# Four more conversion rounds in the second layer's first slices, token forms four steps later, PSUM pools exchanged at the layer border

## The chip, the cores and the metric

The kernel runs on one core of one Trainium2 chip. The metric is the device time in microseconds (us) of one execution of the program. The core's engines are TensorE (PE, with its weight loads shown as PEld), VectorE (DVE), ScalarE (ACT), GpSimd (POOL) and SyncE (SP), which here only issues DMAs. Each engine works through its own instructions in the order in which the program issued them and waits at the head of that queue.

## What is computed

The reference is a causal linear attention with decay, followed by two feed-forward layers over its output:

```python
x = attn_out.transpose(0, 2, 1, 3).reshape(1536, 512)      # 1536 tokens, 512 features
h = x @ moe_w_in                                           # 512 x 2048
g = where(h >= 1, h, where(h <= -1, 0, (h + 1) ** 2 / 4))
x = g @ moe_w_out                                          # 2048 x 512
gate = 1 / (1 + exp(-(x @ moe2_w_gate)))                   # 512 x 1536
out = (gate * (x @ moe2_w_val)) @ moe2_w_out               # 1536 x 512
```

The layers' weights arrive as 64-bit floats.

## The kernel before, in words

**Attention** comes first (16 units, the loop at L910) and writes x as a high and a low part, `xh` and `xl`, so that a product is made of three matmuls: high by high, low weight by high, high weight by low. The 1536 tokens are three groups of 512, t = 0, 1, 2.

**Slices.** The first layer has 16 slices of 128 hidden features (n = 0 to 15), the second has 12 (n = 16 to 27). For a slice, `hidden` (L219, 12 matmuls) makes the hidden features of one token group in a PSUM bank h, ACT and DVE apply the activation, `parts` (L242) splits the result into gh (ACT) and gl (DVE), and `project` (L266, 12 matmuls) adds it to four output accumulators `accs`, one PSUM bank each. After the last slice of a group of slices `flush` (L291) takes the four accumulators into `part[t]` in SBUF, and only then are those banks free. Two pools of four PSUM banks serve this: "a" for the accumulators, "h" for hidden features and products (L958).

**Pairs.** From slice 4 on, slices 4 to 15 and 18 to 27 are worked in pairs n0, n1. Token groups 0 and 1 use a scheme with seven products where there would be eight (`pair_first` L455, `pair` L421; `product` L408 is six matmuls). It needs *token forms*, sums and differences of x (`forms_first` L370: ten DVE additions L381, then four `form_split`, each an ACT copy L367 and a DVE subtraction L368), and *weight forms* s31 and s24 (four additions L149, then `w_forms_split` L152: per form an ACT copy L156 and a subtraction L157). The weight forms are made on DVE in the first layer and on POOL in the second. Token group 2 is done by `hidden`. In the second layer one "pair" iteration (L607) handles the products of slice n0 (a) and n1 (b), projections and the two third-group slices: 14 products, 6 projections and 4 `hidden`, 84 + 72 + 48 = 204 matmuls. The second layer's first two slices, 16 and 17, are done without the scheme, for t = 0, 1, 2 in turn (the loop at L596): per slice and group two `hidden` and one `project`. Between the layers, `x_split` makes xh and xl of the second layer from `part`, and `forms_second` its token forms (DVE, L405).

**Conversion rounds.** There are 68 pieces of weights of 512 columns (two per first-layer slice, three per second-layer slice: two inputs and the output weights at column 1024). `w_round` (L164) is one round k: DVE finishes the bits of piece k-1 (`w_float`, L119, L123), ACT makes the high part of piece k-2 (`w_high`, L127), SP issues a load (`w_load`, L98, 512 KB into three raw buffers), ACT takes the words of piece k apart (`w_words`, L105, L112, L113), DVE makes the low part of piece k-2 (`w_low`, L131) and, where a piece completes a slice's inputs, the weight forms are begun (`w_forms`, L149). Pieces live in ten buffers; a round does nothing while piece k-12 is still needed (L176), nor while forms wait to be split and `prog["room"]` is false (L166). The first action of `w_round` after forms are made is to split them at its end. `w_need` makes rounds on the spot if a weight isn't ready; `pair` and `pair_first` call `w_forms_split` on the spot if forms aren't split (L425, L459). Nothing else paces the rounds: they stand where the program calls them, and that place sets how early a weight is ready.

**Order around the change.** `feed_forward` (L331) yields twice per slice and group. The main program (L961 to L973) takes 16 such steps after attention, and at each of the first 14 pops one entry of the list `made` of `forms_first`. Then come `first_layer` (L488), with three rounds spread over an iteration and one at its end, and `second_layer` (L583). In `second_layer`'s loop `go_on` (L321) runs one entry of `later` and makes a round unless that entry returns True: the rounds made there are two at t = 0, none at t = 1 (the `form_split` calls stand there) and two at t = 2.

Of the kernel before, what the change touches and what calls it, by code (L numbers as in the profile page):

```python
# [26 lines left out]
G0 = 4  # L27
# [13 lines left out]
def fused_kernel(ctx: ExitStack, tc: tile.TileContext, qkv, qd, cst, w1, w2, out):  # L41
# [279 lines left out]
    def go_on():  # L321

        if not (later and later.pop(0)()):
            w_round()
# [45 lines left out]
    def forms_first():  # L370


        at = lambda x, k, t: x[:, k * HK:(k + 1) * HK, t * TT:(t + 1) * TT].bitcast(F32)
        f = {}

        def forming(i, first, *terms):
            def one(k):
                if k == 0:
                    f[i] = fp.tile([P, HK, TT], F32, tag="s", name=f"f{i}")
                op, b_ = terms[k]  # L380
                dve.tensor_tensor(out=f[i], in0=f[i] if k else first, in1=b_() if callable(b_) else b_,  # L381
                                  op=op)
            return [lambda k=k: one(k) for k in range(len(terms))]

        add, sub = ALU.add, ALU.subtract
        both = lambda op, k, t: [(op, at(xh, k, t)), (op, at(xl, k, t))]
        yh, yl = [[at(x, k, 1) for k in range(2)] for x in (xh, xl)]
        return [
            *forming(0, yh[0], *both(sub, 0, 0), (add, yl[0])),
            *forming(3, yh[1], *both(sub, 0, 1), (add, yl[1])),  # L390
            *forming(1, yh[1], (sub, lambda: f[0]), (add, yl[1])),
            *forming(2, at(xh, 1, 0), (sub, lambda: f[1]), (add, at(xl, 1, 0))),
            lambda: form_split(f, 0),
            lambda: form_split(f, 1),
            lambda: form_split(f, 3),
            lambda: form_split(f, 2),
        ]
# [57 lines left out]
    def pair_first(n):  # L455

        w_need(n, 0)
        w_need(n + 1, 0)
        if n not in ready:  # L459
            w_forms_split(n)  # L460
        hw = HK * P
        g, v = ws[index[n, 0]], ws[index[n + 1, 0]]
        s31, s24 = ready[n]
        t_at = lambda i: (xt["h"][:, i], xt["l"][:, i])
        p0, p1, p2 = (bank(f"p{n}_{i}") for i in range(3))
        r = [rest(f"q{n}_{i}") for i in range(3)]
        product(p0, g, 0, x_at(0, 0), True)
        act.activation(r[0], p0, AF.Copy)
        yield
        product(p1, g, hw, x_at(1, 0), True)  # L470
        dve.tensor_tensor(out=r[0], in0=r[0], in1=p1, op=ALU.add)
        yield r
        product(p0, s24, 0, t_at(1), False)
        act.activation(r[1], p0, AF.Copy)
        yield
        product(p2, s31, hw, t_at(0), True)
        yield
        product(p0, s31, 0, x_at(0, 1), False)
        act.activation(r[2], p0, AF.Copy)
        dve.tensor_tensor(out=r[2], in0=r[2], in1=p2, op=ALU.add)  # L480
        yield
        product(p0, v, hw, t_at(2), False)
        yield p0
        product(p2, s24, hw, x_at(1, 1), False)
        dve.tensor_tensor(out=r[1], in0=r[1], in1=p2, op=ALU.add)
        yield

    def first_layer(waiting):  # L488

        square = lambda s: act.activation(s, s, AF.Square)  # L490
        for n0 in range(G0, NF1, GF):
            n1 = n0 + 1
            ending = n1 == NF1 - 1
            a = pair_first(n0)
            next(a)
            r = next(a)
            next(a)
            s11 = act1_begin(r[0], f"s{n0}_0")
            next(a)
            square(s11)  # L500
            next(a)
            act1_end(s11, r[0])
            s22 = act1_begin(r[2], f"s{n1}_1")
            project(*waiting[0], now=False)
            square(s22)
            g11 = parts(s11, n0, 0)
            act1_end(s22, r[2])
            w_round()
            project(*waiting[1], now=False)
            g22 = parts(s22, n1, 1)  # L510
            t_ = waiting[1][:2]
            flush(*t_, (0, 1))
            p0 = next(a)
            flush(*t_, (2, 3))
            s21 = act1_begin(p0, f"s{n1}_0")
            next(a)
            square(s21)
            act1_end(s21, p0)
            s12 = act1_begin(r[1], f"s{n0}_1")
            ha = hidden(n0, 2, 0)  # L520
            used.add(index[n0, 0])
            g21 = parts(s21, n1, 0)
            square(s12)
            act1_end(s12, r[1])
            w_round()
            project(n0, 0, g11, True, False)
            sa = act1(ha, n0, 2)
            act1_end(sa, ha)
            g12 = parts(s12, n0, 1)
            project(n1, 0, g21, False, True)  # L530
            w_round()
            hb = hidden(n1, 2, 0)
            used.add(index[n1, 0])
            if ending:
                x_split(0, (0, 1))
            project(n0, 1, g12, True, False)
            ga = parts(sa, n0, 2)
            sb = act1(hb, n1, 2)
            act1_end(sb, hb)
            gb = parts(sb, n1, 2)  # L540
            project(n1, 1, g22, False, True)
            w_round()
            if ending:
                x_split(0, (2, 3))
            waiting = [(n0, 2, ga, True, False), (n1, 2, gb, False, True)]
        return waiting

# [35 lines left out]
    def second_layer(waiting):  # L583

        x_split(1, range(4))
        f = forms_second()
        for p in waiting:
            project(*p)
        later.extend([
            lambda: x_split(2, (0, 1)),  # L590
            lambda: x_split(2, (2, 3)),
            lambda: form_split(f, 0) or form_split(f, 2) or True,
            lambda: form_split(f, 1) or form_split(f, 3) or True,
        ])
        fresh = None
        for t in range(NTT):  # L596
            for n in range(NF1, NF1 + GF):
                r = single(n, t)
                if fresh:
                    behind.append(fresh[:2] + (parts(fresh[2], *fresh[:2]),) + fresh[3:])  # L600
                if len(behind) == 2:
                    project(*behind.pop(0))
                fresh = n, t, r, n == NF1, n == NF1 + GF - 1
                go_on()
        behind.append(fresh[:2] + (parts(fresh[2], *fresh[:2]),) + fresh[3:])
        waiting = behind
        for n0 in range(NF1 + GF, NF1 + NF2, GF):  # L607
            n1 = n0 + 1
            a, b = pair(n0), pair(n1)
            next(a)  # L610
            w_round()
            for _ in range(4):
                next(a)
            prog["room"] = False
            for p in waiting:
                w_round()
                project(*p, now=False)
            flush(p[0], p[1], (0, 1))
            ra, ga = next(a), {}
            flush(p[0], p[1], (2, 3))  # L620
            prog["room"] = True
            xa = pair_act(n0, ra, ga)
            for _ in range(5):
                next(b)
                next(xa)
            w_round()
            project(n0, 0, ga[0], True, False)
            w_round()
            rb, gb = next(b), {}
            ha = single(n0, 2, pair_act(n1, rb, gb))  # L630
            w_round()
            project(n1, 0, gb[0], False, True)
            ha = parts(ha, n0, 2)
            w_round()
            hb = single(n1, 2)
            w_round()
            project(n0, 1, ga[1], True, False)
            hb = parts(hb, n1, 2)
            project(n1, 1, gb[1], False, True)
            waiting = [(n0, 2, ha, True, False), (n1, 2, hb, False, True)]  # L640
        for p in waiting:
            project(*p)
# [313 lines left out]
    with tc.manual_schedule():  # L956
        psx.close()
        for c in "ah":  # L958
            banks[c] = ctx.enter_context(
                tc.tile_pool(name=f"ps{c}", bufs=4, space=PSUM, reuse_waits="tile"))  # L960
        made = forms_first()  # L961
        for _ in steps:
            if made:
                made.pop(0)()
        while len(behind) > 2:
            project(*behind.pop(0))
            go_on()
        assert not made
        prog["split"] = True
        waiting = first_layer(list(behind))  # L970
        behind.clear()
        prog["forms"] = pool
        second_layer(waiting)  # L973
# [61 lines left out]
```

## Time and profile before

| | |
|---|---|
| median of 3 runs | 634.1 us (634.02 to 634.88) |
| the profiled execution | 634.59 us, of which the span from first to last instruction is 632.8 us |
| busy in the span | PE 95%, PEld 77%, DVE 69%, ACT 61%, POOL 17% |
| mean granted TensorE clock | 0.975 of full speed |
| chain that ended last | PE 82%, DVE 9%, ACT 4%, POOL 2%, issue 1% |

The span is read here in stretches: attention ends near 65 us, the first layer's slices 0 to 3 reach to 117 us, its pairs to 306 us, the second layer's first two slices go from 313 to 356 us, and its five pairs from there to the end, one every 51.6 us. A row of the timeline gives the start, the duration, the engine, the line, the operation, the tiles (output first) and a count of merged instructions; in brackets stands the idle time just before it and what ended that. The duration of a matmul in a row contains its passage through the array, so the distance between starts is the cost of one in a row of many.

### The profile page before, as it was taken

How to read it: one execution, taken by the hardware profiler on the slowest of the kernel's cores; microseconds unless marked ns; L12 is line 12 of the kernel's file. 1: busy time of each engine (PE TensorE's matmuls, PEld its weight loads, DVE VectorE, ACT ScalarE, POOL GpSimd, SP SyncE). 2: the span in 40 equal slices, each digit the busy share in tenths (PEclk: the TensorE clock that was granted, in tenths of full speed). 3: DMA queues.
4: the chain of work that ended last, by engine and by line, in shares of the span. 5: the costliest groups of instructions: out<-in, count | busy, mean ns of one | idle time of the engine just before them, and what ended most of it. 6: DMA issues, size and time to landing. Idle time of an engine off the chain costs nothing.

```text
span 632.8 us, 7957 instructions
## 1 busy us (share of the span) xinstructions
PE 602.1 (95%) x2980; PEld 488.4 (77%) x2980; DVE 435.4 (69%) x734; ACT 383.8 (61%) x678; POOL 108.0 (17%) x116
## 2 busy tenths in 40 slices
PE   8999999999999999999999797997999799799797
PEld 5887878788888888888788576886888688688686
DVE  6789797687878787878995434665574584475544
ACT  6798656795868686868664455654553654564320
POOL 4389400000000000000000240060052043025000
PEclk8999999999999999999999987999899899899899
DMA  8992410121111111222220122220320231200013
GB/s 286 403 346 89 160 62 1 67 68 66 67 68 67 67 66 67 67 67 66 68 66 8 60 67 67 67 66 1 100 73 27 67 100 34 66 34 1 0 67 133
DMA packets 15813, 52.58 MB, mean 83 GB/s; under 512 B 1688, under 2 KB 2976, under 8 KB 15776
## 3 DMA queue, kind: packets, MB, share of 16 engines
q1 hardware_dynamic: 15760, 52.08, 23.8%
q8 instruction: 23, 0.38, 0.2%
q14 instruction: 14, 0.11, 0.1%
q10 hardware_dynamic: 16, 0.01, 0.0%
HBM read 48.92 MB, written 3.15 MB: 82 GB/s over the span
## 4 chain that ended last, share of the span: by engine, by line
PE 82%; DVE 9%; ACT 4%; POOL 2%; issue 1%; DMA 0%; ACTq 0%; POOLq 0%; DVEq 0%
PE a L281 32%; PE p L414 23%; PE h L226 7%; PE h L227 7%; PE h L228 7%; PE s L795 2%; PE x L877 2%; PE x L868 1%; DVE part L303 1%; DVE w L131 1%; PE uu L810 1%; DVE gl L246 1%; DVE f L381 1%; DVE wr L119 1%; DVE wr L123 1%
## 5 line engine op out<-in xcount | busy, mean ns | idle before, releaser
L281 PE MATMUL a<-gh,w 128*128 128x512 f32 x384 | 118.8, 390 | 2.1 <-DVE part L301 1.2
L281 PE MATMUL a<-w,gh 128*128 128x512 f32 x288 | 96.7, 416 | 16.2 <-ACT w L127 8.9
L149 POOL TENSOR_TENSOR wr<-wr 128x256 f32<-128x256 f32 x20 | 16.4, 821 | 441.2 <-DVE w L131 440.5
L303 DVE TENSOR_TENSOR part<-part,a 128x512 f32<-128x512 f32 x132 | 83.1, 681 | 12.3 <-PE a L281 12.3
L226 PE MATMUL h<-xh,w 128*128 128x512 f32 x224 | 87.7, 391 | 0.0
L227 PE MATMUL h<-xh,w 128*128 128x512 f32 x224 | 87.2, 389 | 0.0
L228 PE MATMUL h<-xl,w 128*128 128x512 f32 x224 | 87.2, 389 | 0.0
L281 PEld LDWEIGHTS a<-gh,w 128*128 128x128 f32 x384 | 71.8, 188 | 18.3 <-DVE part L301 1.6
L281 PEld LDWEIGHTS a<-w,gh 128*128 128x128 f32 x288 | 57.7, 200 | 32.1 <-ACT w L127 11.0
L281 PE MATMUL a<-gl,w 128*128 128x512 f32 x192 | 74.7, 389 | 0.0
L281 PE MATMUL a<-w,gl 128*128 128x512 f32 x144 | 59.4, 413 | 0.0
L226 PEld LDWEIGHTS h<-xh,w 128*128 128x128 f32 x224 | 42.1, 188 | 9.0
L228 PEld LDWEIGHTS h<-xl,w 128*128 128x128 f32 x224 | 42.1, 188 | 8.8
L227 PEld LDWEIGHTS h<-xh,w 128*128 128x128 f32 x224 | 42.0, 188 | 8.6
L414 PE MATMUL p<-xth,s 128*128 128x512 f32 x128 | 42.1, 409 | 5.8 <-ACT q L434 4.8
L131 DVE TENSOR_TENSOR w<-wr,w 128x512 fp32r<-128x512 f32 x61 | 44.6, 731 | 4.2 <-ACT w L127 4.1
L127 ACT ACTIVATE w<-wr 128x512 fp32r<-128x512 f32 x68 | 42.3, 622 | 7.9 <-DVE wr L123 5.0
L123 DVE CUSTOM_DVE_ANT_0 wr<-wr,wc 128x1024 uint16<-128x1024 uint16 x60 | 44.0, 734 | 3.9 <-ACT wc L113 1.6
L112 ACT ACTIVATE wc<-raw 128x512 uint16<-128x512 uint32 x59 | 45.9, 778 | 0.0
L113 ACT ACTIVATE wc<-raw 128x512 f16<-128x512 f32 x59 | 45.2, 766 | 0.0
L105 ACT ACTIVATE wr<-raw 128x512 f32<-128x512 f32 x68 | 44.9, 660 | 0.0
L245 ACT ACTIVATE gh<-r 128x512 fp32r<-128x512 f32 x40 | 25.0, 626 | 30.4 <-DVE r L262 22.4
(117 smaller groups left out, 1088.7 us busy)
## 6 DMA issues: line engine op xcount, KB each, us to landing
raw<-in_w SPq DMA_DIRECT2D x68, 512.0 KB, 3.4
u<-in_qkv SPq DMA_DIRECT2D x12, 768.0 KB, 7.5
u<-in_qkv SPq DMA_DIRECT2D x8, 384.0 KB, 6.5
out<-part SPq DMA_DIRECT2D x12, 256.0 KB, 2.1
DT<-pd SPq DMA_DIRECT2D x1, 256.0 KB, 4.8
qp<-pd SPq DMA_DIRECT2D x2, 96.0 KB, 4.8
DT<-pd SPq DMA_DIRECT2D x1, 128.0 KB
cs<-in_cst SPq DMA_DIRECT2D x1, 98.0 KB, 2.0
```

What stands on the lines that cost most here:

```text
L105: act.activation(r, hi.bitcast(F32), AF.Copy, scale=2.0 ** -112)
L112: act.activation(limb(U16)[:, :, 0], lo, AF.Copy, scale=2.0 ** -29)
L113: act.activation(limb(F16)[:, :, 1], hi.bitcast(F32), AF.Copy, scale=2.0 ** -60)
L123: eng.tensor_tensor(out=ri, in0=ri, in1=c, op=ALU.add)
L127: act.activation(ws[i][:, 0], tmps[i][0], AF.Copy)
L131: eng.tensor_tensor(out=ws[i][:, 1], in0=r, in1=ws[i][:, 0].bitcast(F32), op=ALU.subtract)
L226: pe.matmul(h, lhsT=wh, rhs=xh[:, k, tt], start=(k == 0), stop=False)
L227: pe.matmul(h, lhsT=wl, rhs=xh[:, k, tt], start=False, stop=False)
L228: pe.matmul(h, lhsT=wh, rhs=xl[:, k, tt], start=False, stop=(k == NP - 1))
L281: pe.matmul(accs[j], lhsT=a, rhs=b_, start=(first and m == 0), stop=(last and m == 2))
L303: dve.tensor_tensor(out=o, in0=o, in1=accs[j], op=ALU.add)
L414: pe.matmul(o, lhsT=a, rhs=b_, start=(start and k == 0 and m == 0), stop=(k == HK - 1 and m == 2), skip_group_check=True)
```

## The change

- In the main program the first four steps pop nothing from `made`. The list has one entry more, `w_forms_split(G0)` for the first pair, before the last two; what the steps leave is popped down to two entries, and these two (`form_split(f, 3)`, `form_split(f, 2)`) are popped inside the first iteration of `first_layer`, after its first and second product. `pair_first` no longer splits weight forms itself.
- In the last iteration of `first_layer` the third round is left out, and at its end the pools "a" and "h" change places, so that accumulators take the banks that hidden features used, and the other way round.
- In the loop over the second layer's first two slices a round is made after `go_on` for t = 1 and t = 2, four in all.

```diff
@@ forms_first
             lambda: form_split(f, 0),
             lambda: form_split(f, 1),
+            lambda: w_forms_split(G0),
             lambda: form_split(f, 3),
             lambda: form_split(f, 2),
@@ pair_first
         w_need(n + 1, 0)
-        if n not in ready:
-            w_forms_split(n)
@@ first_layer
-    def first_layer(waiting):
+    def first_layer(waiting, made):
...
             next(a)
+            if made:
+                made.pop(0)()
             r = next(a)
+            if made:
+                made.pop(0)()
             next(a)
...
             project(n1, 0, g21, False, True)
-            w_round()
+            if not ending:
+                w_round()
             hb = hidden(n1, 2, 0)
...
             if ending:
                 x_split(0, (2, 3))
+                banks["a"], banks["h"] = banks["h"], banks["a"]
@@ second_layer
                 go_on()
+                if t:
+                    w_round()
@@ main program
-        for _ in steps:
-            if made:
+        for i, _ in enumerate(steps):
+            if i >= 4 and made:
                 made.pop(0)()
-        while len(behind) > 2:
-            project(*behind.pop(0))
-            go_on()
-        assert not made
+        assert len(behind) == 2
+        while len(made) > 2:
+            made.pop(0)()
         prog["split"] = True
-        waiting = first_layer(list(behind))
+        waiting = first_layer(list(behind), made)
```

## Rows read from the trace of the kernel before

**Rows 1.** The page, busy time, share of the span and instructions of each engine:

```profile
PE 602.1 (95%) x2980; PEld 488.4 (77%) x2980; DVE 435.4 (69%) x734; ACT 383.8 (61%) x678; POOL 108.0 (17%) x116
```

**Rows 2.** Waits: who waited for whom, total us, times, longest us:

```profile
PE a L281 <- ACT w L127: 8.9, 5, 1.8
```

**Rows 3.** Timeline of PE, the wait in the middle of pair 18:

```profile
387.76 0.50 PE L281 MATMUL a<-w,gh 128*128 128x512 f32 x1 [1.78 <-ACT w L127]
389.71 0.80 PE L281 MATMUL a<-w,gh 128*128 128x512 f32 x1 [1.45 <-DVE w L131]
...
395.85 0.65 PE L414 MATMUL p<-xth,w 128*128 128x512 f32 x2
```

**Rows 4.** Windows: stretch, length, busy time (instructions) by engine, granted clock, DMA share, GB/s:

```profile
392.00:394.00 2.00, 2.00 (x6) 1.61 (x5) 0.00 (x0) 0.00 (x0) 0.00 (x0) 0.50 0.66 193
```

**Rows 5.** Chain that ended last, the projections that end pair 18 and pair 20:

```profile
411.69 5.44 PE a L281 x24
...
463.32 5.44 PE a L281 x24
```

**Rows 6.** Timeline of PE, the third product of pair 18:

```profile
364.04 0.80 PE L414 MATMUL p<-xth,s 128*128 128x512 f32 x1 [4.80 <-ACT q L434]
365.36 0.79 PE L414 MATMUL p<-xth,s 128*128 128x512 f32 x1 [0.52 <-POOL s L157]
...
368.51 0.43 PE L414 MATMUL p<-xtl,s 128*128 128x512 f32 x1
```

**Rows 7.** Timeline of ACT, the same place, from the last round of slice 17 on:

```profile
356.37 0.62 ACT L127 ACTIVATE w<-wr 128x512 fp32r<-128x512 f32 x1
...
358.73 0.61 ACT L245 ACTIVATE gh<-r 128x512 fp32r<-128x512 f32 x1
...
362.87 0.63 ACT L156 ACTIVATE s<-wr 128x512 fp32r<-128x512 f32 x1 [1.36 <-POOL wr L149]
363.41 0.58 ACT L434 ACTIVATE q<-p 128x512 f32<-128x512 f32 x1
```

**Rows 8.** Timeline of PE, the layer border and the fourth hidden of slices 16, 17:

```profile
306.18 0.39 PE L281 MATMUL a<-gl,w 128*128 128x512 f32 x1
307.28 0.70 PE L281 MATMUL a<-gh,w 128*128 128x512 f32 x2 [0.71 <-DVE part L303]
...
321.00 0.39 PE L226 MATMUL h<-xh,w 128*128 128x512 f32 x1
```

**Rows 9.** Timeline of DVE, the layer border up to the second round of the second layer:

```profile
300.99 0.42 DVE L119 TENSOR_SCALAR wr<-wr 128x512 uint32<-128x512 uint32 x1
...
302.65 1.29 DVE L313 TENSOR_TENSOR xl<-part,xh 128x512 fp32r<-128x512 f32 x2
...
306.45 2.48 DVE L303 TENSOR_TENSOR part<-part,a 128x512 f32<-128x512 f32 x4
...
324.30 0.68 DVE L131 TENSOR_TENSOR w<-wr,w 128x512 fp32r<-128x512 f32 x1
```

**Rows 10.** Timelines of PE and DVE, the first projection of token group 1:

```profile
85.10 0.73 PE L281 MATMUL a<-gh,w 128*128 128x512 f32 x2 [0.21 <-ACT part L299]
87.92 0.73 PE L281 MATMUL a<-gh,w 128*128 128x512 f32 x2 [1.16 <-DVE part L301]
...
86.04 1.22 DVE L381 TENSOR_TENSOR f<-xh 128x1024 f32<-128x1024 f32 x1
```

**Rows 11.** Timelines of PE and ACT, the first pair's third product:

```profile
119.88 0.90 PE L414 MATMUL p<-xth,s 128*128 128x512 f32 x2 [0.40 <-ACT q L468]
...
109.90 1.04 ACT L367 ACTIVATE xth<-f 128x1024 fp32r<-128x1024 f32 x1
```

**Rows 12.** Timelines of DVE and POOL while POOL makes forms:

```profile
364.54 1.32 DVE L131 TENSOR_TENSOR w<-wr,w 128x512 fp32r<-128x512 f32 x1 [2.28 <-ACT w L127]
...
362.80 2.50 POOL L157 TENSOR_TENSOR s<-wr,s 128x512 fp32r<-128x512 f32 x2
```

**Rows 13.** The page's DMA issues: KB each, median us to landing:

```profile
raw<-in_w SPq DMA_DIRECT2D x68, 512.0 KB, 3.4
```

## Prediction, made before the changed kernel ran

> **What bounds the kernel now.** I read the busy table first: PE is busy 95% of the span [rows 1], so the time is PE's work plus its waits, and only a change of those waits can pay. The rate comes from the chain of waits: 24 matmuls in 5.44 us [rows 5], 0.2267 us from start to start. Pair 18 and pair 20 end their projections 463.32 - 411.69 = 51.63 us apart [rows 5], while 204 matmuls at that rate are 46.25 us. So 5.38 us of each pair are no matmul work. The table of waits names a place: five times, once a pair, the projection `a` waits for ACT's `w_high` L127 [rows 2]. In the timeline it stands in the middle of the pair: 1.78 us for the high part of the output weights, one matmul, 1.45 us for the low part from DVE [rows 3]; and right behind it the windows show a granted clock of 0.50 [rows 4], the lower of the two levels (1.2 instead of 2.4 GHz). From 387.76 to 395.85 there are 15 matmuls, 3.40 us of work in 8.09. So a wait of 3.2 us costs its length and the slow stretch behind it.
>
> Why there: round k finishes piece k-2. Counting the calls in program order, round 44, which finishes piece (18, 1024), is called one line ahead of the projection that needs it, and likewise in every later pair; the weight forms of n1 are split on the spot, too. The rounds are about four too late for the whole second layer.
>
> **D, the five waits in the pairs.** I counted the rounds of the changed program call by call: one fewer before the border, four more in the loop of slices 16 and 17, and a round in pair 18 that is now not refused for want of room. Round 44 moves from the middle of pair 18 into the last (slice, group) step of that loop, and round 50, which finishes (20, 1024), from the middle of pair 20 into pair 18 behind its first third-group slice. From there to the use are 96 and 156 matmuls (22 and 35 us), and no weight form is split on the spot any more. No round is refused for a buffer; the nearest is round 50, whose piece 38 is marked used just ahead of it. What goes: four times 5.38, and in pair 18, where the slow stretch is longer, 8.09 - 3.40 + 1.78 + 0.16 (restart) = 6.63 [rows 3]: **-28.2 us**.
>
> What is late next in a pair: the same ACT queue. From the end of b's fifth product ACT has a copy of a product and a sigmoid (0.5 each from start to start, as L156 ahead of L434 [rows 7]), a round (358.73 - 356.37 = 2.36 [rows 7]), two form copies (0.54 each, same rows), and a second round of 2.36, whose L105 needs a buffer that POOL frees by the two subtractions of 2.50 [rows 12]. POOL begins at about 4.0 and ends at 6.5, three ACT operations of 0.6 follow, then gh of n1 at about 9. PE has 12 + 12 + 24 matmuls until it needs that gh, 10.88 us. Margin 1.9 us, so nothing new. SP's loads move with their rounds: two rounds back to back are 4.7 us, a load is issued two rounds ahead and lands in 3.4 [rows 13].
>
> **C, the first products of pair 18.** Here PE waits 4.80 us for L434, the copy of p0, then 0.52 for POOL's split, and is slow until 368.51 [rows 6]: eight matmuls from 364.04 take 4.47 instead of 1.81, so 4.96 + 2.66 = 7.6 us in all. L434 stands on ACT behind the two form copies L156, the second of which waited for POOL until 362.87 [rows 7]. After the change forms 18 are done earlier, but forms 19 are now made in that same round at 356.37, and split one round later, still ahead of L434. POOL's work starts at the same place, the second L156 again goes at 362.87, then gh of slice 17 (0.54), which was ahead of it, then L434: 0.5 us later than before. The second round's 2.36 on ACT lies inside the wait for POOL. The 0.52 goes. So the wait stays: **0 us**, though the step might seem made to remove it.
>
> **B, the layer border.** (1) The exchange of the pools removes the wait of 0.71 us for the accumulators of the last group [rows 8]; 307.28 - 306.18 less one matmul is **-0.87**, and the restart 0.09: -0.96. (2) The round left out (302.65 - 300.99 = 1.66 us of DVE [rows 9]) moves every later piece one round back. Round 37, which finishes (17, 512), was the last of the first layer; it becomes the first of the second, at the place of round 38, whose L131 ends at 324.30 + 0.68 = 324.98 [rows 9]. Between 306.45 and there DVE had no idle time, so the end follows the start of the four L303. These can begin 1.66 earlier as far as DVE goes, but their last needs the projection's last matmul (306.18 + 0.39) and ends at 307.3 instead of 308.84: 1.54 earlier. So the low part of (17, 512) is ready at 323.4. PE wants it for the second matmul of slice 17's second `hidden`, which started at 321.00 [rows 8]: now 320.04, plus 0.23. A new wait of 323.5 - 320.27 = **+3.2**. It is as long as the pair's 1.78 + 1.45, so it should bring a slow stretch as that does: behind the wait the later pairs lose 5.38 - 3.23 - 0.16 = 2.0 more, pair 18 8.09 - 3.40 - 1.45 = 3.2 [rows 3, 5]. I take **+2.0**, as four of the five pairs have it; the bounds are 0 (the clock holds) and 3.2. The next weight, (16, 1024), has 1.4 us to spare by the same count. B in sum: +4.2.
>
> The extra rounds themselves: at t = 1 ACT carries a sigmoid, gh, two form copies of 1.04 [rows 11] and a round of 2.36 in a step of 36 matmuls, 8.16 us; at t = 2 two rounds, two copies of 0.54, sigmoid, gh: 7 to 8.3. Cover is PE's 8.16. It fits with one step of delay, and PE's next consumer of ACT is a step later; cost 0, and up to 1 us if that cover fails.
>
> **A, token forms.** The wait of 0.21 + 1.16 at 85 to 88 us is for the copies L299 and L301 that free the accumulators; on DVE four form additions of 1.22 stood ahead of them [rows 10]. With no forms in the first four steps the copies are done in time: from 85.10 to 87.92 six matmuls took 2.82 instead of 1.36, and 0.21 + 0.16 lie ahead: **-1.8**. The same list is now late at its other end: two form splits, not one, stand on ACT in the full stretch ahead of L468 (1.04 each [rows 11], 0.95 from start to start). The wait of 0.40 grows to about 1.4: **+1.0**. The two entries popped inside the first pair are ahead of PE's use by 1 us and more. A: -0.8.
>
> **A rule against the change.** While POOL works on forms, L131 took 1.32 us on DVE [rows 12] where it takes 0.68 [rows 9]. With POOL's work moved into steps where DVE also flushes, I lay 0.6 us on each of three DVE operations ahead of gh: 1.9 us, just the margin above; ACT, not DVE, is the later of the two there, so the sum keeps 0. The Trainium skill, "SBUF — State Buffer", section "Who interferes with whom", says that a DVE instruction with two SBUF inputs contends with a GpSimd instruction that reads SBUF. For L131 the trace agrees, by those two numbers; by that rule, with POOL slowed by DVE as well, the sum would be that of rival 2, otherwise it stays.
>
> **Sum.** -28.2 + 0 + 4.2 - 0.8 = -24.8 against the profiled execution's 634.59, so 609.8. That execution lies 0.49 above the median of the runs shown; against 634.1 it is **609.3 us**.
>
> **Rivals.** (1) *The two waits that I keep are not there*: B's new wait is covered (609.3 - 5.2 = 604.1), or C's goes (609.3 - 7.6 = 601.7); both together give 596.5. For it: both rest on ACT and DVE queues counted to 1 us. Against: the before trace has DVE without a gap at the border [rows 9]. (2) *POOL becomes the gate in the pairs*: while DVE and POOL hold each other up, gh of n1 comes 2 us too late in each of five pairs, +10: 619.3. For it: 1.9 us of margin. Against: POOL is busy 17% [rows 1]. (3) *The lead doesn't hold, and the change is slower*: if the extra rounds do nothing, since a round returns while piece k-12 is still needed, D's gain is nil and B's price stays: 634.1 + 4.2 - 0.8 = 637.5. It decides if even four rounds between 39 and 50 are refused. Against: by my count none is. This is also the case in which the change doesn't do what it says.
>
> **Numbers.** Forecast 0.62 (604.5 to 612, by B's clock and 1 us for each cover), rival 1 0.22, rival 2 0.10, rival 3 0.03, the rest 0.03 spread over other waits that return part of D. For 8 in 10 the range reaches to 600 (most of rival 1) and to 616: half of rival 2. A measurement can tell about 0.2% (1.3 us) from no change: faster 0.96, same 0.01, slower 0.03 (rival 3).
>
> **What would show it.** Right: pairs 46.3 us apart, no wait of PE for `w` L127 in the pairs, clock 1.00 there; PE still waits near 5 us for L434 in pair 18; no wait for L303 at the border, but about 3 us for L131 in slice 17's second `hidden`; no wait for L301 near 87 us, one of about 1.4 for L468. Wrong: pairs still 51 us apart, or any repeated wait of PE on `gh` or POOL.

## The result, and the profile after

The changed kernel took **609.73 us** (607.49 to 610.37 in four runs) beside 634.4 us (634.02 to 634.88) for the kernel before on the same chip, a ratio of 0.9604 with a 95% interval of 0.9579 to 0.963. The forecast was 609.3 us in a range of 600 to 616. The profiled execution took 609.95 us, 24.64 less than the 634.59 of the one before; the sum on record was -24.8. Of the five executions behind the 597.37 us near the end of this document, the profiled one took 984.13 us at a mean granted clock of 0.558, and the ratio given there leaves it out.

The top of the page shows no engine with fewer instructions; the matmuls are the same 2980, and PE's share of the span rose from 95 to 97% [rows 1], in a span of 608.2 us where it was 632.8. PE's busy time itself fell by 11.8 us: a matmul in a stretch at the lower clock counts as busy for longer (0.63 us at 322.98, 0.39 at 326.70), so the 95% of before held a part of the loss.

```profile
PE 590.3 (97%) x2980; PEld 482.8 (79%) x2980; DVE 442.3 (73%) x734; ACT 381.6 (63%) x678; POOL 110.0 (18%) x116
```

The table of PE's waits (waiter and what it waited for: total us, times, longest us) answers to [rows 2]. The five waits for `w` L127 are gone, and the wait that the prediction kept and the one that it added now lead the list. L435 is the L434 of before.

```profile
PE p L415 <- ACT q L435: 5.4, 1, 5.4
PE h L227 <- DVE w L131: 3.0, 1, 3.0
```

The chain that ended last gives the new rate of the pairs, from the projection that ends pair 18 to the one that ends pair 20 [rows 5]: 454.76 - 408.52 = 46.24 us, where 204 matmuls need 46.25.

```profile
408.52 5.44 PE a L281 x24
...
454.76 5.44 PE a L281 x24
```

The windows (stretch, its length, busy us and instructions of PE, PEld, DVE, ACT, POOL, then the granted clock, DMA share, GB/s) show where the lower clock level is left: behind the wait for L131 and behind the wait for L435. In the last 208 us the clock is full; the stretch of [rows 4] has no successor.

```profile
322.00:325.00 3.00, 2.62 (x6) 2.14 (x7) 0.33 (x1) 3.00 (x6) 0.00 (x0) 0.52 0.46 156
...
368.00:372.00 4.00, 4.00 (x11) 3.13 (x10) 2.90 (x5) 2.32 (x4) 0.12 (x1) 0.50 0.31 70
400.00:608.00 208.00, 204.36 (x902) 168.95 (x900) 129.16 (x196) 94.41 (x165) 41.88 (x39) 1.00 0.17 54
```

PE's timeline, in order of time, shows the three waits that are left after attention, with matmuls around them (L467 is the L468 of before):

```profile
118.97 0.91 PE L415 MATMUL p<-xth,s 128*128 128x512 f32 x2 [1.36 <-ACT q L467]
...
318.99 0.41 PE L226 MATMUL h<-xh,w 128*128 128x512 f32 x1
322.38 0.80 PE L227 MATMUL h<-xh,w 128*128 128x512 f32 x1 [2.98 <-DVE w L131]
...
325.54 0.40 PE L228 MATMUL h<-xl,w 128*128 128x512 f32 x1
...
367.38 1.22 PE L415 MATMUL p<-xth,s 128*128 128x512 f32 x2 [5.39 <-ACT q L435]
...
373.66 0.63 PE L415 MATMUL p<-xh,s 128*128 128x512 f32 x2
```

*At the border* the second `hidden` of slice 17 starts at 318.99, waits 2.98 us for its second matmul, and takes 3.16 us for the next seven (322.38 to 325.54), which at 0.2267 are 1.59. The chain of waits in that stretch is DVE: in the 5 us ahead of the matmul it adds to `part`, multiplies a slice's values by their gate (L582), makes two `xl`, and then does the round (L119, L123) whose L131 PE needs, with hardly a gap.

```profile
316.99 1.88 DVE part L303 x3
318.86 0.60 DVE r L582
319.46 1.20 DVE xl L313 x2
...
321.73 0.61 DVE w L131
...
322.38 0.80 PE h L227
```

*In pair 18* the wait is on ACT. Its timeline shows two rounds in a row (two L127, each followed by its L105, L112 and L113), then the two form copies L156, the second held 1.29 us by POOL's additions, and only then gh and the copy L435 for which PE stands still:

```profile
359.13 0.62 ACT L127 ACTIVATE w<-wr 128x512 fp32r<-128x512 f32 x1
...
361.49 0.61 ACT L127 ACTIVATE w<-wr 128x512 fp32r<-128x512 f32 x1
...
363.80 0.61 ACT L156 ACTIVATE s<-wr 128x512 fp32r<-128x512 f32 x1
365.70 0.63 ACT L156 ACTIVATE s<-wr 128x512 fp32r<-128x512 f32 x1 [1.29 <-POOL wr L149]
366.23 0.61 ACT L245 ACTIVATE gh<-r 128x512 fp32r<-128x512 f32 x1
366.75 0.58 ACT L435 ACTIVATE q<-p 128x512 f32<-128x512 f32 x1
```

The sum, as the two profiles have it, is taken up behind the experiments.

### The profile page after: what moved, and what is told of

Same layout as the page of the kernel before. It is cut to its first block, busy times and chain, and to the rows that moved or that the text cites. A ratio compares the mean times of both kernels' runs of the same rounds, so it can differ in the third digit from the quotient of the medians.

```text
span 608.2 us, 7963 instructions
## 1 busy us (share of the span) xinstructions
PE 590.3 (97%) x2980; PEld 482.8 (79%) x2980; DVE 442.3 (73%) x734; ACT 381.6 (63%) x678; POOL 110.0 (18%) x116
## 4 chain that ended last, share of the span: by engine, by line
PE 85%; DVE 6%; DMA 4%; ACT 3%; POOL 1%; issue 1%; SPq 0%; POOLq 0%
PE a L281 33%; PE p L415 24%; PE h L227 8%; PE h L226 8%; PE h L228 8%; DMA u<-in_qkv 2%; DMA raw<-in_w 2%; DVE part L303 2%; PE x L884 1%; PE s L802 1%; DVE xl L313 1%; PE x L875 1%; DVE part L406 1%; POOL wr L149 1%; DVE gl L246 1%
## 5 line engine op out<-in xcount | busy, mean ns | idle before, releaser
L303 DVE TENSOR_TENSOR part<-part,a 128x512 f32<-128x512 f32 x132 | 83.3, 681 | 12.4 <-PE a L281 12.4
L281 PE MATMUL a<-w,gh 128*128 128x512 f32 x288 | 88.7, 389 | 0.0
L281 PEld LDWEIGHTS a<-w,gh 128*128 128x128 f32 x288 | 54.1, 188 | 11.2
L281 PE MATMUL a<-w,gl 128*128 128x512 f32 x144 | 56.0, 389 | 0.0
L131 DVE TENSOR_TENSOR w<-wr,w 128x512 fp32r<-128x512 f32 x61 | 46.7, 766 | 5.1 <-ACT w L127 5.1
L105 ACT ACTIVATE wr<-raw 128x512 f32<-128x512 f32 x68 | 45.1, 664 | 4.6 <-POOL s L157 3.6
L123 DVE CUSTOM_DVE_ANT_0 wr<-wr,wc 128x1024 uint16<-128x1024 uint16 x60 | 43.6, 727 | 4.3 <-ACT wc L113 1.8
L112 ACT ACTIVATE wc<-raw 128x512 uint16<-128x512 uint32 x59 | 46.1, 782 | 0.0
L127 ACT ACTIVATE w<-wr 128x512 fp32r<-128x512 f32 x68 | 42.3, 621 | 5.4 <-POOL wr L123 2.8
L113 ACT ACTIVATE wc<-raw 128x512 f16<-128x512 f32 x59 | 45.4, 769 | 0.0
L157 POOL TENSOR_TENSOR s<-wr,s 128x512 fp32r<-128x512 f32 x20 | 29.9, 1515 | 81.2 <-ACT s L156 81.2
```

Source lines behind the costliest of these rows:

```text
L105: act.activation(r, hi.bitcast(F32), AF.Copy, scale=2.0 ** -112)
L112: act.activation(limb(U16)[:, :, 0], lo, AF.Copy, scale=2.0 ** -29)
L113: act.activation(limb(F16)[:, :, 1], hi.bitcast(F32), AF.Copy, scale=2.0 ** -60)
L123: eng.tensor_tensor(out=ri, in0=ri, in1=c, op=ALU.add)
L127: act.activation(ws[i][:, 0], tmps[i][0], AF.Copy)
L131: eng.tensor_tensor(out=ws[i][:, 1], in0=r, in1=ws[i][:, 0].bitcast(F32), op=ALU.subtract)
```

## Experiments

The theory: the four extra rounds are the whole gain (D), the round left out at the border is a loss (B), the first products of pair 18 keep their wait (C), the token forms are worth about a microsecond (A). The rivals: that the border's parts (round and pools) carry some of the gain, and that POOL stands close to being the gate in the pairs. All times below are medians, each beside runs of the kernel before on the same chip.

### The four rounds alone

The kernel before with one edit, so that border, pools and token forms stay as they were:

```diff
@@ second_layer
                 go_on()
+                if t:
+                    w_round()
```

> The kernel before with the four extra rounds alone. Theory (the rounds make the gain, the other parts cost more than they bring): the five waits in the pairs go, -28.4 us; the border stays as it was before, with the wait of 0.7 us for L303 and no wait for L131 in slice 17; the wait for L434 in pair 18 is about 4.3 us plus 2 us of slow clock instead of 7.6. 634.4 - 28.4 - 1.3 = 604.7 us, faster than the whole change. Rival (the round left out at the border and the exchanged pools make room that the extra rounds need): 609.7 us or more, with new waits between 306 and 330 us.

Measured: **605.49 us** (603.87 to 607.24), ratio 0.9545 (0.9522 to 0.9567). Two lines of the changed kernel alone make more than the whole change, by about 4 us; so the rest of it must cost that much on balance. The chain that ended last has pair 18 and pair 20 at the distance of the changed kernel, 449.49 - 403.25 = 46.24 us:

```profile
403.25 5.44 PE a L281 x24
...
449.49 5.44 PE a L281 x24
```

PE's timeline keeps the border's wait for L303 and has a wait of 3.98 for L434, shorter than the 4.80 before [rows 6]. In the window from 365 to 602 us PE is busy 234.09 of 237.00 us at a granted clock of 1.00.

```profile
307.31 0.70 PE L281 MATMUL a<-gh,w 128*128 128x512 f32 x2 [0.72 <-DVE part L303]
...
363.25 0.90 PE L414 MATMUL p<-xth,s 128*128 128x512 f32 x2 [3.98 <-ACT q L434]
```

### The border: the round put back, the pools not exchanged, and both

Three kernels, each the changed one with part of its border undone. The first keeps the round:

```diff
@@ first_layer
-            if not ending:
-                w_round()
+            w_round()
```

> The changed kernel with the third round of the first layer's last iteration put back. Theory: the wait of 3.0 us for L131 in slice 17 and its slow stretch (1.6 us) go, the wait for L434 in pair 18 falls to about 4.3 us, with 2 us of slow clock: 609.7 - 4.7 - 2.1 = 602.9 us. Rival (DVE is full at the border, so that its 1.7 us come back as another wait there): 607 to 610 us.

Measured: **602.53 us** (602.45 to 603.13), ratio 0.9501 (0.9485 to 0.9516). PE waits neither for L131 nor for L303 here. And the wait of pair 18 is shorter:

```profile
361.05 1.00 PE L415 MATMUL p<-xth,s 128*128 128x512 f32 x2 [3.99 <-ACT q L435]
...
365.49 0.61 PE L415 MATMUL p<-xh,s 128*128 128x512 f32 x2
```

The reason is in ACT's timeline of this kernel: the two form copies stand between the rounds and in one piece, with no wait for POOL, where the changed kernel's second copy waited 1.29 us. From the L127 of the first of the two rounds to L435 it is 360.43 - 354.20 = 6.23 us here and 366.75 - 359.13 = 7.62 there.

```profile
356.56 1.13 ACT L156 ACTIVATE s<-wr 128x512 fp32r<-128x512 f32 x2
...
360.43 0.57 ACT L435 ACTIVATE q<-p 128x512 f32<-128x512 f32 x1
```

So leaving the round out costs twice. At the border it costs 2.98 + 0.16 (restart) + 1.57 (slow) = 4.7 us. At pair 18, where every piece is one round late, the loss falls from 8.43 us (5.39 + 0.16 + 2.88) to 5.87 when the round is back: 3.99 + 0.16 and twelve matmuls in 365.49 - 361.05 = 4.44 us that would take 2.72. Together 7.3; the medians differ by 7.2, and by the ratios it is 6.5.

The second leaves the pools in place, with the round still left out:

```diff
@@ first_layer
                 x_split(0, (2, 3))
-                banks["a"], banks["h"] = banks["h"], banks["a"]
```

> The changed kernel without the exchange of the two PSUM pools. Theory: with the round left out the flush before the border starts 1.5 us earlier, so no wait for L303 is there to be removed and the exchange brings nothing: 609.7 us within 0.5, PE's wait for L131 in slice 17 still 3.0 us. Rival (the exchange is what removes the wait of 0.7 us for L303): that wait is back, and the later one is 2.1 instead of 3.0 us, since PE comes to it later; the time is nearly the same, and the two waits tell them apart.

Measured: 609.66 us (608.08 to 612.43), ratio 0.9615 (0.9583 to 0.9646), beside 609.73. The exchange makes no difference in the changed kernel. PE has no wait for L303 in this one either: without the round the banks are free in time. The wait for L131 is the same to the hundredth:

```profile
324.63 0.73 PE L227 MATMUL h<-xh,w 128*128 128x512 f32 x1 [2.98 <-DVE w L131]
```

The third undoes both, which is the changed kernel with the border of before:

```diff
@@ first_layer
-            if not ending:
-                w_round()
+            w_round()
...
                 x_split(0, (2, 3))
-                banks["a"], banks["h"] = banks["h"], banks["a"]
```

> The changed kernel with the border as before: the third round of the last iteration is put back and the pools are not exchanged. Beside e2 (602.5 us, the round put back, the pools exchanged) this shows the exchange alone. Theory: with that round in place PE waits 0.7 us for L303 again, so the exchange is worth 0.9 to 1.0 us: 603.5 us. Rival (the exchange never matters): 602.5 us, no wait for L303.

Measured: 603.51 us (603.23 to 604.56), ratio 0.9501 (0.9485 to 0.9517). The ratio equals that of the kernel with the round and the exchange, since the two ran on chips whose runs of the kernel before differ by 0.55 us (634.47 and 635.02); the times alone do not settle a microsecond. PE's timeline does: the wait is back.

```profile
305.98 0.70 PE L281 MATMUL a<-gh,w 128*128 128x512 f32 x2 [0.71 <-DVE part L303]
```

The border's wait for L303 thus has two cures, either of which is enough: the exchange, for which these runs show no price, and the missing round, which costs about 7 us elsewhere. The change applies both.

This last kernel and the four rounds alone differ in the token forms and nothing else. They took 603.51 and 605.49 us, ratios of 0.9501 and 0.9545, so here the token forms bring 2.0 us by the medians and 2.8 by the ratios.

### The last of the four rounds left out

```diff
@@ second_layer
                 go_on()
-                if t:
+                if t and (n, t) != (NF1 + 1, 2):
                     w_round()
```

> The changed kernel with three extra rounds: the one of slice 17 at t = 2 is left out, so that the forms of slice 19 are split behind L434 and not ahead of it. Theory: PE's wait for L434 in pair 18 falls from 5.4 to about 0.8 us, a wait of about 1.3 us for L440 follows, the clock stays: 609.7 - 8.4 + 2.1 = 603.4 us, pairs still 46.3 us apart with three rounds of lead. Rival (four rounds of lead are needed): waits of PE for L127 or L131 return in the pairs, up to 5.4 us each, 609 us or more.

Measured: **603.43 us** (602.47 to 603.66), ratio 0.9509 (0.9495 to 0.9523). Three extra rounds do for the pairs what four do (pair 18 and pair 20 end 448.20 - 401.96 = 46.24 us apart), and the wait of pair 18 nearly goes. In ACT's timeline one round stands ahead of the copy L435, and the form copies, their wait for POOL with them, come behind it, where they delay only the next product's copy, L441:

```profile
361.45 0.59 ACT L435 ACTIVATE q<-p 128x512 f32<-128x512 f32 x1
...
365.14 0.63 ACT L156 ACTIVATE s<-wr 128x512 fp32r<-128x512 f32 x1 [0.25 <-POOL wr L149]
365.68 0.58 ACT L441 ACTIVATE q<-p 128x512 f32<-128x512 f32 x1
```

PE's timeline and the window over these two waits: 0.64 and 1.21 us, and the granted clock stays full.

```profile
362.09 0.73 PE L415 MATMUL p<-xth,s 128*128 128x512 f32 x2 [0.64 <-ACT q L435]
...
366.31 0.73 PE L415 MATMUL p<-xh,s 128*128 128x512 f32 x2 [1.21 <-ACT q L441]
```

```profile
363.00:367.00 4.00, 2.79 (x13) 2.00 (x12) 3.22 (x4) 3.00 (x6) 3.84 (x5) 1.00 0.56 186
```

The extra round that comes last is therefore the one that keeps C's wait. In the changed kernel it puts two things in front of L435 on ACT: its own work, 363.80 - 361.49 = 2.31 us, and the form split behind it, 366.23 - 363.80 = 2.43 us, of which 1.29 are a wait for POOL. Together they are 4.74 us, and PE's wait fell by 5.39 - 0.64 = 4.75. No run takes away the split and leaves the round; the kernel with the border's round put back has both in front of L435 without the wait for POOL, and still waits 3.99 us.

### The token forms alone

The kernel before with the edits of the token forms and nothing else; the core of them is

```diff
@@ main program
-        for _ in steps:
-            if made:
+        for i, _ in enumerate(steps):
+            if i >= 4 and made:
                 made.pop(0)()
```

> The kernel before with the later token forms alone. Theory: the wait of 1.4 us for L299 and L301 near 85 us goes with its restarts (-1.9 us), the wait for L467 near 119 us grows from 0.4 to 1.4 us (+1.0): 634.4 - 0.9 = 633.5 us, the rest as before. Rival (the forms are merely late at another place): no difference.

Measured: 633.95 us (632.77 to 635.29, 12 runs) beside 635.02 (17 runs), ratio 0.9978 (0.9967 to 0.9989). That is -1.1 by the medians and -1.4 by the ratio: a gain, and a small one. PE's timeline has no wait for L299 or L301 [rows 10], and the wait at the first pair has grown from 0.40 [rows 11] to 1.36, while the waits in the pairs stay as they were:

```profile
118.12 0.91 PE L415 MATMUL p<-xth,s 128*128 128x512 f32 x2 [1.36 <-ACT q L467]
...
386.07 0.50 PE L281 MATMUL a<-w,gh 128*128 128x512 f32 x1 [1.78 <-ACT w L127]
```

### POOL as the gate: its subtractions made three times

To find how far the changed kernel is from rival 2, each of POOL's subtractions of the weight forms in the second layer is repeated in place, with the same values:

```diff
@@ w_forms_split
-            prog["forms"].tensor_tensor(...)
+            for _ in range(3 if prog["forms"] is pool else 1):
+                prog["forms"].tensor_tensor(...)
```

> The changed kernel with each of POOL's subtractions L157 made three times, the same values each time. It prices the second rival of the prediction, POOL as the gate of the pairs. In the changed kernel ACT's L105 waits 0.9 us for the first subtraction and gh of n1 ends 2.2 us ahead of PE's need. Theory: the first form takes 5.3 instead of 1.8 us, gh of n1 comes 3.5 us later, and PE waits for it about 1.2 us in each pair, with up to 2 us more behind it: 616 to 625 us. Rival (POOL has room to spare): 609.7 to 611 us.

Measured: **620.2 us** (619.76 to 620.82), ratio 0.9758 (0.9741 to 0.9776), 10.5 us over the changed kernel (9.8 by the ratios). PE's waits show what the prediction named as the sign of this rival, a wait for gh (here L561) once in each of the four pairs that still split forms, and the growth of C:

```profile
PE p L416 <- ACT q L436: 8.4, 1, 8.4
...
PE a L282 <- ACT gh L561: 2.9, 4, 0.7
```

POOL's six subtractions take 9.27 us in pair 20 of this kernel. In the changed kernel the two take 3.54:

```profile
444.80 9.27 POOL L158 TENSOR_TENSOR s<-wr,s 128x512 fp32r<-128x512 f32 x6 [15.29 <-ACT s L156]
```

So 5.7 us more on POOL become 0.7 us of PE's wait at gh. In all it is some 2.1 us a pair: PE's waits for gh end at 403.86 and 452.25 us, 48.39 us apart, where a pair took 46.24. The margin itself is read in the changed kernel. In pair 20 ACT's round waits 0.90 us for POOL (L105), gh of n1 ends at 443.59 + 0.62 = 444.21, and PE takes it at 446.44: 2.2 us to spare.

```profile
441.75 0.68 ACT L105 ACTIVATE wr<-raw 128x512 f32<-128x512 f32 x1 [0.90 <-POOL s L157]
...
443.59 0.62 ACT L560 ACTIVATE gh<-q 128x512 fp32r<-128x512 f32 x1
```

```profile
446.44 0.62 PE L281 MATMUL a<-w,gh 128*128 128x512 f32 x2
```

### Both losses taken out

The changed kernel with the border's round back, with the last step of slices 16 and 17 without any round, and with two of the token forms made together in steps 6 and 8, which was to clear the first pair's start:

```diff
@@ first_layer
-            if not ending:
-                w_round()
+            w_round()
@@ second_layer
-                go_on()
-                if t:
-                    w_round()
+                if (n, t) != (NF1 + 1, 2):
+                    go_on()
+                    if t:
+                        w_round()
@@ main program
-            if i >= 4 and made:
-                made.pop(0)()
+            for _ in range(2 if i in (6, 8) else i >= 4):
+                if made:
+                    made.pop(0)()
```

> A version made from the theory: the changed kernel with the third round of the last iteration put back, no rounds at all in the last step of slices 16 and 17 (so that nothing stands on ACT ahead of L435), and two of the token forms' entries popped in each of steps 6 and 8. Theory: no wait for L131 in slice 17 (-4.7 us), none for L435 and about 0.7 us for L441 in pair 18 (-7.7 us), no wait for L467 near 118 us (-1.5 us), no slow clock after the start: 609.7 - 13.9 = 595.8 us. Rival (these waits only hide others, since ACT and DVE have no room): 600 us or more.

Measured: **597.37 us**, ratio 0.9398 (0.9383 to 0.9413). The same kernel was run once more for its profile:

> The version of e6 once more, to read its waits. Theory: PE waits for none of L299, L301, L467, L303, L131 and L435; about 0.7 us for L441 in pair 18 and nothing else over 0.5 us after attention; clock 1.00 after the first 20 us: 596 to 597.5 us. Rival (a wait has only moved): a wait of 1 us or more at a place where the changed kernel had none.

Measured: **596.89 us** (596.02 to 599.63), ratio 0.9394 (0.9356 to 0.9433). It is the best version found, about 13 us under the change and 38 under the kernel before. Two lines of its page (busy times; the granted clock in 40 slices of the span, in tenths, 9 for 90% or more), then PE's waits for ACT:

```profile
PE 585.3 (98%) x2980; PEld 479.6 (81%) x2980; DVE 444.0 (75%) x734; ACT 381.1 (64%) x678; POOL 110.8 (19%) x116
...
PEclk9999999999999999999999999999999999999999
```

```profile
PE p L415 <- ACT q L467: 1.0, 1, 1.0
...
PE p L415 <- ACT q L441: 0.5, 1, 0.5
```

The waits for L131 and L435 are gone, and the granted clock is 1.00 in the mean of the whole span. One expectation failed: the first pair's wait for L467 is 0.96, not 0. ACT's timeline gives the reason. It is full from 106.26 to the copy at 117.43, with two form copies and the weight forms' split in it that the earlier pops did not move out:

```profile
107.52 1.04 ACT L367 ACTIVATE xth<-f 128x1024 fp32r<-128x1024 f32 x1
...
111.34 1.14 ACT L156 ACTIVATE s<-wr 128x512 fp32r<-128x512 f32 x2
...
113.62 1.04 ACT L367 ACTIVATE xh<-f 128x1024 fp32r<-128x1024 f32 x1
...
117.43 0.58 ACT L467 ACTIVATE q<-p 128x512 f32<-128x512 f32 x1
```

## Why the prediction was right, point by point

| term | predicted, us | measured, us | from |
|---|---|---|---|
| D, five waits in the pairs | -28.2 | -28.2 | period 46.24, no wait in the pairs |
| C, first products of pair 18 | 0 | +0.8 | wait 5.39 + 0.16, slow 2.88; before 7.6 |
| B, the border | +4.2 | +3.8 | -0.96, wait 2.98 + 0.16, slow 1.57 |
| A, token forms | -0.8 | -0.9 | waits of 1.9 gone, 1.0 new |
| sum | -24.8 | -24.5 | the profiled executions differ by 24.64 |

The forecast of 609.3 us lies 0.4 us from the 609.73 measured. Part of that is luck: the price of C was put 0.8 us too low and that of B 0.4 us too high, so that the two errors partly cancel.

**D** was right in size and cause. The period of a pair fell from 51.63 to 46.24, four times 5.39, and pair 18 lost its 6.63. The four rounds alone, with the pairs 46.24 us apart, show that these calls did it. That a returning round would refuse the lead (rival 3, the slower one) is excluded by the same row: the lead holds to the end. The prediction did not see that four extra rounds are more than is needed; three suffice.

**C** is the term that was mis-sized. The prediction had the wait stay because the form split still stands ahead of the copy on ACT. That mechanism holds as far as the order on ACT goes; the kernel without the last extra round takes away the split and the round together, so the share of each is read from ACT's rows and not tested alone. The step "0.5 us later than before. The 0.52 goes" came out as well: the wait grew by 0.59 to 5.39, and the 0.52 is gone. What failed is that the slow stretch behind it was taken to stay the same. Before, 2.66 us were lost behind the first wait, 0.52 of them in the second wait, so 2.14 in slow matmuls; now fifteen matmuls from 367.38 to 373.66 took 6.28 us instead of 3.40, 2.88 lost. The kernel without the exchange of the pools repeats it, with 2.99 lost behind the same wait of 5.39. The windows give a granted clock of 0.50 from 372 to 373 us and 0.84 from 373 to 374.

**B** was right in mechanism, with 0.4 us too much for the slow stretch: 1.57 lost, where +2.0 was taken from the later pairs and the bounds were 0 and 3.2. The new wait, 2.98 and 0.16 for the restart, was predicted as 3.2. Two things that the prediction did not say: the exchange of the pools, to which it gave the removal of the wait for L303, is worth nothing beside the left-out round, since either does it (the prediction's own 1.54 us, by which the flush ends earlier, already cover the 0.71 us of that wait); and the left-out round costs 2.6 us more at pair 18, which the sum had inside C's unchanged wait. That is why the four rounds alone beat the change.

**A** came out as two small amounts of opposite sign, as worked out; measured alone it is -1.1 to -1.4, with an interval that leaves out zero, and -2.0 to -2.8 beside the four rounds.

**The rivals.** Rival 1 did not happen, but its arithmetic did: the kernel without both waits, which it put at 596.5, ran at 596.9 (that kernel also has the shorter wait at the first pair). Rival 2 was priced by the experiment with three subtractions: it needs 5.7 us more of POOL's work to give 10.5 us, and the margin is 2.2 us where the prediction had 1.9. That this is so near is in part luck: the prediction let ACT's L105 wait for two subtractions of 2.50 us together, while in pair 20 the two take 3.54 us and L105 waits for the first alone. POOL's two subtractions took 2.50 us in pair 18 before [rows 12] and 3.54 in pair 20 of the changed kernel, here in POOL's timeline:

```profile
439.89 3.54 POOL L157 TENSOR_TENSOR s<-wr,s 128x512 fp32r<-128x512 f32 x2 [19.35 <-ACT s L156]
```

The Trainium skill ("SBUF — State Buffer", section "Who interferes with whom") would have DVE work with two SBUF inputs and GpSimd work reading SBUF contend. DVE's L131 fits it, with 1.38 us beside these subtractions in pair 20 and 0.68 us at 438.72 ahead of them. How much of the step from 2.50 to 3.54 comes from it is open: L131 runs beside both, and no run here isolates a cause. The margin absorbed it.

The cause of the spread between executions was not looked for. In the changed kernel the shortest time has the highest mean granted clock (607.49 us at 0.996, 610.37 at 0.989), but in the four rounds alone it has not (603.87 us at 0.994, 607.24 at 0.997).

## What to carry to other kernels

Find each conversion's place in program order and count from there to its first use; a whole layer that runs a fixed number of calls late is cured by a few calls made earlier, once. Then check each added call for what it pulls ahead of a copy that PE waits for: a round, and above all a step that itself waits for another engine, is better placed behind that copy than in front of it in the same queue. And undo the parts of a change one at a time even when the sum comes out as forecast, since here two parts of it gave back most of 13 us of a possible 38.

## What the runs showed of the hardware that was not expected

The cost of a wait of PE is not proportional to it, because of the clock behind it. Waits of 0.64, 1.21 and 1.36 us cost their length and a restart of 0.3 to 0.5 us (the matmuls around them, from start to start): the windows that hold them (363 to 367 us without the last round, 118 to 122 us in the changed kernel) show a granted clock of 1.00. Behind a wait of 2.98 the matmuls lost 1.57 us (322.38 to 325.54, clock 0.52), behind 3.99 they lost 1.72, behind 5.39 they lost 2.88. At 8.45 (the kernel with three subtractions) the loss had hardly grown: fifteen matmuls took 6.42 us, 3.02 lost. The length of the wait alone does not settle the loss, though. Behind the same 1.78 and 1.45 us in the kernel before, fourteen matmuls of pair 18 lost 6.14 - 3.17 = 2.97 us [rows 3], and in each of the four later pairs the slow stretch lost only 1.6 to 1.7. What decides between the two no run here shows.

```profile
370.02 1.22 PE L416 MATMUL p<-xth,s 128*128 128x512 f32 x2 [8.45 <-ACT q L436]
...
376.44 0.62 PE L416 MATMUL p<-xh,s 128*128 128x512 f32 x2
```
